# Where the second MoE splits its token operands: between the output products, or one pair ahead inside the first product

## The chip, the cores and the metric

The kernel runs on one core of one Trainium2 chip. The metric is the device time of one execution in microseconds (us), the median of several runs. Engines are named as the profile names them: PE is TensorE (PEld its weight loads), DVE is VectorE, ACT is ScalarE, POOL is GpSimd, SP is SyncE, whose queue issues most of the transfers.

## The reference

```python
x = masked_attention(q, k, v)                  # 4 x 8 heads, 576 positions, 64 wide; as 2304 tokens x 512
h = x @ w_in;  x = (h - np.tanh(h)) @ w_out    # first MoE: 512 -> 2048 -> 512
h = x @ w_in2                                  # second MoE: 512 -> 1024
e = np.exp(h - h.max(-1, keepdims=True))
solu = h * e / (e.sum(-1, keepdims=True) + 1e-09)
ln = (solu - mean(solu)) / np.sqrt(var(solu) + 1e-06) * g_ln
out = ln @ w_out2                              # 1024 -> 512, float32
```

Everything is float32. The kernel keeps that precision on TensorE by writing each operand as a high and a low part in a rounded format (`fp32r`) and adding three products: high x high, high x low, low x high.

## The kernel before, in words

The program is one stream per engine, written out in order; each engine runs its own stream in that order, and a wait of one instruction holds everything behind it on the same engine.

**First MoE.** 2304 tokens are six groups of 384; a slot `s` is one of 16 blocks of the hidden width of a group. In slot `s` TensorE does `mm1` (12 matmuls into a bank `h`, of which there are two) and `mm2` of five slots earlier (12 matmuls into the four banks `y`). ACT does the tanh (L362), VectorE the subtraction `t` (L365), which frees the bank `h`, ACT the high part `gs` (L368), VectorE the low part (L371). At the end of a group `y` goes to a DRAM buffer `y_dr`.

In the last group (slots NS-NF to NS-1, sixteen of them) the weights of the second MoE are prepared beside this, one block per slot: a load (L444), ACT's `top` (L449), VectorE's `f` (L457), ACT's high part (L473), VectorE's low part (L479). GpSimd makes four differences of weight blocks per half (L467, in two steps of two); they belong to a scheme that needs seven products of blocks in place of eight.

**The split of tokens.** A pair is 256 tokens, two tiles of 128; there are nine. `load_y(j)` fetches the pair `j` from `y_dr` into `yr` (one buffer). `split_y(j)` prepares the operands `yt` (two buffers): GpSimd makes three sums and differences `ysm` and overwrites one quarter of `yr` with a fourth (L530), VectorE casts the high parts (L535: `yr` first tile, `yr` second tile, `ysm`), GpSimd subtracts for the low parts (L536, one behind each cast). The second cast reads the quarter that the fourth addition writes. Pairs 0 and 1 are split during the last group of the first MoE, the others between the output products.

**Second MoE.** `mm3(i)` is the first product of a pair: seven blocks of 6 matmuls (`sp`, L618), in banks `b0` to `b3`. ACT copies `b0` to `c` (L650); VectorE adds `u2` (L651, from `b1` and `c`) and `u3` (L656, from `b3` and `u2`) and combines them with later banks into the negated `hn` of each tile (L634). The sixth block, `b21`, overwrites the bank `b3` that `u3` reads, so it waits for `u3`. Then, per tile, the odd one first: exponential (ACT, L678), product (VectorE, L683), mean and its subtraction (L689, L690), and `fac`: ACT's Square (L697) and six small operations on GpSimd (L699 to L704) that give the row factor `f`.

`trz` transposes a tile's `hn` on TensorE into two banks `zt` (L714, 8 matmuls); ACT copies the high part `zh` (L716), VectorE subtracts for the low part `zl` (L717), which frees the bank. `mm4` is the output product (`po`, L727, 24 matmuls), scaled by `f` in ACT's `o` (L730) and stored (L731).

The order of the main loop for pair `i` is: split of pair i+2, load of pair i+3, `mm4` odd, `trz` odd of pair i+1, `mm4` even, `trz` even of pair i+1, `mm3(i+2)`. The first two pairs differ: `mm3(0)` and `mm3(1)` follow each other, and `trz` of both tiles of pair 0 stands inside `mm3(1)` (its `mid`).

## Time and profile before

| | |
|---|---|
| median of 3 runs | 734.07 us (731.76 to 735.8) |
| the profiled execution's own time | 735.53 us |
| its span | 733.7 us |
| PE busy | 702.3 us (96%) |
| PEld | 645.5 us (88%) |
| DVE | 459.3 us (63%) |
| ACT | 367.7 us (50%) |
| POOL | 185.6 us (25%) |

The profile and the trace are of one execution, and its rows are in microseconds from the start of its span. A busy share says little by itself here: TensorE is never far from busy, so what matters is where it waits, and on whom. A matmul's shown length holds the drain of the pipeline, so lengths of neighbouring rows overlap a little; differences of starts do not have that fault. A row of the windows view gives, for each engine, the busy time in a stretch and the number of instructions, then the granted clock of TensorE (1.00 is 2.4 GHz, 0.50 is 1.2 GHz). A row of a timeline ends with the idle time ahead of it and who ended it, where there was any.

### The profile page before, as it was taken

How to read it: one execution, taken by the hardware profiler on the slowest of the kernel's cores; microseconds unless marked ns; L12 is line 12 of the kernel's file. 1: busy time of each engine (PE TensorE's matmuls, PEld its weight loads, DVE VectorE, ACT ScalarE, POOL GpSimd, SP SyncE). 2: the span in 40 equal slices, each digit the busy share in tenths (PEclk: the TensorE clock that was granted, in tenths of full speed). 3: DMA queues.
4: the chain of work that ended last, by engine and by line, in shares of the span. 5: the costliest groups of instructions: out<-in, count | busy, mean ns of one | idle time of the engine just before them, and what ended most of it. 6: DMA issues, size and time to landing. Idle time of an engine off the chain costs nothing. (4 is left out here: it accounts for less than half of the span.)

```text
span 733.7 us, 11467 instructions
## 1 busy us (share of the span) xinstructions
PE 702.3 (96%) x4106; PEld 645.5 (88%) x4106; DVE 459.3 (63%) x1157; ACT 367.7 (50%) x917; POOL 185.6 (25%) x253
## 2 busy tenths in 40 slices
PE   6888999999999999999999999899999999999997
PEld 5688899999999999999999999899778777877786
DVE  5987676476676667776666335969665545554550
ACT  5778775465556555555554334544343234323431
POOL 2212311011110101111111101743263456345620
PEclk9999999999999999999999999899999999999999
DMA  9985521132223222212130016332101110111001
GB/s 273 339 271 177 181 69 54 64 109 65 66 65 108 66 66 65 90 55 64 64 108 1 1 58 205 125 115 88 44 0 58 57 58 1 58 59 58 29 15 43
DMA packets 30312, 64.03 MB, mean 87 GB/s; under 512 B 2992, under 2 KB 16816, under 8 KB 30256
## 3 DMA queue, kind: packets, MB, share of 16 engines
q1 hardware_dynamic: 27088, 58.59, 25.3%
q10 hardware_dynamic: 3168, 4.72, 1.8%
q8 instruction: 32, 0.52, 0.3%
q14 instruction: 24, 0.20, 0.1%
HBM read 53.86 MB, written 9.44 MB: 86 GB/s over the span
## 5 line engine op out<-in xcount | busy, mean ns | idle before, releaser
L354 PE MATMUL h<-x,wi 128*128 128x384 f32 x1152 | 223.7, 343 | 4.4 <-DVE t L365 4.3
L381 PE MATMUL y<-gs,wo 128*128 128x384 f32 x1152 | 219.2, 340 | 0.0
L354 PEld LDWEIGHTS h<-x,wi 128*128 128x128 f32 x1152 | 200.7, 190 | 6.4 <-DVE t L365 5.3
L381 PEld LDWEIGHTS y<-gs,wo 128*128 128x128 f32 x1152 | 201.6, 190 | 1.8
L253 POOL TENSOR_TENSOR p<-p,rs 96x512 f32<-96x512 f32 x47 | 57.3, 1219 | 352.0 <-DVE rs L251 330.2
L371 DVE TENSOR_TENSOR gs<-t,gs 128x384 fp32r<-128x384 f32 x96 | 78.8, 821 | 42.4 <-ACT gs L368 42.3
L727 PE MATMUL po<-w2o_o,z 128*128 128x512 f32 x432 | 102.6, 394 | 0.0
L365 DVE TENSOR_TENSOR t<-h,t 128x384 f32<-128x384 f32 x96 | 53.0, 552 | 70.6 <-ACT t L362 70.6
L727 PEld LDWEIGHTS po<-w2o_o,z 128*128 128x128 f32 x432 | 80.5, 188 | 17.3
L362 ACT ACTIVATE t<-h 128x384 f32<-128x384 f32 x96 | 46.8, 488 | 82.8 <-PE h L354 79.7
L245 ACT ACTIVATE p<-p,nm 96x128 f32<-96x128 f32 x192 | 75.1, 393 | 21.3 <-DVE nm L210 21.0
L368 ACT CAST gs<-t 128x384 fp32r<-128x384 f32 x96 | 48.6, 507 | 46.7 <-DVE t L365 46.6
L678 ACT ACTIVATE e<-hn,sml 128x1024 f32<-128x1024 f32 x18 | 20.8, 1153 | 67.1 <-DVE sml L634 50.5
L618 PE MATMUL sp<-w2i_t,yt 128*128 128x512 f32 x216 | 52.4, 396 | 0.9 <-DVE u L651 0.9
L618 PEld LDWEIGHTS sp<-w2i_t,yt 128*128 128x128 f32 x216 | 40.4, 188 | 11.0 <-DVE u L651 1.4
L618 PE MATMUL sp<-w2i_b,yt 128*128 128x512 f32 x162 | 41.2, 399 | 0.0
L535 DVE CAST yt<-yr 128x512 fp32r<-128x512 f32 x18 | 15.0, 843 | 37.3 <-POOL yr L530 37.3
L205 PE MATMUL qkp<-qkr 64*96 64x128 f32 x160 | 29.4, 339 | 7.3 <-DMA qkr<-in_qk_dram 5.4
L245 ACT ACTIVATION_READ_ACCUMULATOR p<-p,nm 96x1 f32 x192 | 36.3, 189 | 0.0
L618 PEld LDWEIGHTS sp<-w2i_b,yt 128*128 128x128 f32 x162 | 29.8, 188 | 6.5
L205 PEld LDWEIGHTS qkp<-qkr 64*96 64x96 f32 x160 | 24.1, 205 | 11.9 <-DMA qkr<-in_qk_dram 5.8
L730 ACT ACTIVATE o<-po,sml 128x512 f32<-128x512 f32 x18 | 12.2, 679 | 42.8 <-POOL yt L536 25.0
(82 smaller groups left out, 845.0 us busy)
## 6 DMA issues: line engine op xcount, KB each, us to landing
qkr<-in_qk_dram SPq DMA_DIRECT2D x28, 448.0 KB, 3.3
raw_wi<-in_w_in_dram SPq DMA_DIRECT2D x16, 511.8 KB, 7.2
raw_wo<-in_w_out_dram SPq DMA_DIRECT2D x16, 511.8 KB, 7.0
v<-in_vw_dram SPq DMA_DIRECT2D x48, 128.0 KB, 3.4
y_dr<-ys ACTq DMA_DIRECT2D x6, 768.0 KB, 3.9
yr<-y_dr SPq DMA_DIRECT2D x9, 512.0 KB, 4.5
out_dram<-o SPq DMA_DIRECT2D x18, 256.0 KB, 4.5
qkr<-in_qk_dram SPq DMA_DIRECT2D x20, 224.0 KB, 4.5
```

The lines of the kernel that those rows point to most:

```text
L205: nc.tensor.matmul(ps[:, b], d["r"][:64, b * NQ:(b + 1) * NQ], d["r"][:64, QC + b * NK:QC + (b + 1) * NK], start=True, stop=True)
L245: nc.scalar.activation(out=d["p"][:, b], in_=d["p"][:, b], func=AF.Exp, scale=-1.0, bias=d["nm"][:, b:b + 1], accum_out=d["sm"][:, b:b + 1])
L253: eng.tensor_tensor(out=d["p"], in0=d["p"], in1=d["rs"].unsqueeze(2).to_broadcast([NQ, 4, NK]), op=ALU.mult)
L354: nc.tensor.matmul(ps, w[:, a, k * 128:(k + 1) * 128], xt[g, k][:, b], start=(n == 0), stop=(n == 3 * KD - 1))
L362: nc.scalar.activation(out=t, in_=ps, func=AF.Tanh)
L365: nc.vector.tensor_tensor(out=t, in0=ps, in1=t, op=ALU.subtract)
L368: nc.scalar.copy(out=gs[:, 0], in_=t)
L371: nc.vector.tensor_tensor(out=gs[:, 1], in0=t, in1=gs[:, 0].bitcast(F32), op=ALU.subtract)
L381: nc.tensor.matmul(yb[g][m], wo[c][:, a, m * 128:(m + 1) * 128], gs[:, b], start=(c == 0 and i == 0), stop=(c == NF - 1 and i == 2))
L618: nc.tensor.matmul(ps, y[:, a, blk, kk], w2i[w, kk][:, b], start=first and q == 0, stop=q == 5, skip_group_check=not first)
L678: nc.scalar.activation(out=d["e"], in_=d["hn"], func=AF.Exp, bias=d["sml"][:, 0:1], scale=-1.0, accum_out=d["sml"][:, 1:2])
L727: nc.tensor.matmul(po, z[:, a, j], w2o[j][:, b], start=(q == 0), stop=(q == 3 * NF2 - 1))
```

## The change

1. In the last group of the first MoE, the load of pair 0 moves to the group's start and its split from slot 7 to slot 3; the split of pair 1 moves from slot 14 to slot 8. Each is followed by the load of the next pair.
2. `split_y` takes parts. From pair 2 on, a pair is split inside the first product of the pair ahead of it: part 0 (three additions, cast and low part of the first tile) behind the second block, parts 1 and 2 (fourth addition, the other two casts and low parts) behind `u2`, and then the load of the next pair. The low part of the first tile now stands ahead of the fourth addition on GpSimd. In the main loop the split is gone.
3. `fac` is taken out of `softmax_z`. That of the odd tile stays where it was; that of the even tile is issued behind `trz` of the odd tile, so its Square stands on ACT behind the odd tile's `zh`.

```diff
--- before.py
+++ after.py
@@ -507,7 +507,7 @@
 
     w2_plan()
 
-    yt, y_raw = {}, {}
+    yt, y_raw, y_sm = {}, {}, {}
 
     NP = NTOK // YT
 
@@ -516,25 +516,31 @@
             y_raw[j] = p2.tile([128, KD, YT], F32, tag="yr", name=f"yr{j}", bufs=1)
             nc.sync.dma_start(out=y_raw[j], in_=y_dr[:, :, j * YT:(j + 1) * YT])
 
-    def split_y(j):
+    def split_y(j, parts=range(3)):
 
         if j >= NP:
             return
-        r = y_raw.pop(j)
-        y = p2.tile([128, 2, 7, 2, TT], F32R, tag="yt", name=f"yt{j}")
-        sm = p2.tile([128, 3, 2, TT], F32, tag="ysm", name=f"ysm{j}", bufs=1)
-        a11, a12 = r[:, 0:2, 0:TT], r[:, 2:4, 0:TT]
-        a21, a22 = r[:, 0:2, TT:YT], r[:, 2:4, TT:YT]
-        for o, a, b, op in ((sm[:, 0], a21, a22, ALU.add), (sm[:, 1], sm[:, 0], a11, ALU.subtract),
-                            (sm[:, 2], a11, a21, ALU.subtract), (a21, a12, sm[:, 1], ALU.subtract)):
-            nc.gpsimd.tensor_tensor(out=o, in0=a, in1=b, op=op)
+        r = y_raw[j]
+        if 0 in parts:
+            y = yt[j] = p2.tile([128, 2, 7, 2, TT], F32R, tag="yt", name=f"yt{j}")
+            sm = y_sm[j] = p2.tile([128, 3, 2, TT], F32, tag="ysm", name=f"ysm{j}", bufs=1)
+            a11, a21, a22 = r[:, 0:2, 0:TT], r[:, 0:2, TT:YT], r[:, 2:4, TT:YT]
+            for o, a, b, op in ((sm[:, 0], a21, a22, ALU.add), (sm[:, 1], sm[:, 0], a11, ALU.subtract),
+                                (sm[:, 2], a11, a21, ALU.subtract)):
+                nc.gpsimd.tensor_tensor(out=o, in0=a, in1=b, op=op)
+        y, sm = yt[j], y_sm[j]
+        if 1 in parts:
+            nc.gpsimd.tensor_tensor(out=r[:, 0:2, TT:YT], in0=r[:, 2:4, 0:TT], in1=sm[:, 1], op=ALU.subtract)
         yh = y[:, 0].rearrange("p s k t -> p (s k) t")
         yl = y[:, 1].rearrange("p s k t -> p (s k) t")
-        for sl, v in ((slice(0, 4), r[:, :, 0:TT]), (slice(4, 8), r[:, :, TT:YT]),
-                      (slice(8, 14), sm.rearrange("p s k t -> p (s k) t"))):
-            nc.vector.tensor_copy(out=yh[:, sl], in_=v)
-            nc.gpsimd.tensor_tensor(out=yl[:, sl], in0=v, in1=yh[:, sl].bitcast(F32), op=ALU.subtract)
-        yt[j] = y
+        for p, sl, v in ((0, slice(0, 4), r[:, :, 0:TT]), (2, slice(4, 8), r[:, :, TT:YT]),
+                         (1, slice(8, 14), sm.rearrange("p s k t -> p (s k) t"))):
+            if p in parts:
+                nc.vector.tensor_copy(out=yh[:, sl], in_=v)
+                nc.gpsimd.tensor_tensor(out=yl[:, sl], in0=v, in1=yh[:, sl].bitcast(F32), op=ALU.subtract)
+        if 2 in parts:
+            y_raw.pop(j)
+            y_sm.pop(j)
 
 
     p2 = None
@@ -555,6 +561,7 @@
             p2 = tc.alloc_tile_pool(name="p2", bufs=2, side="right", reuse_waits="tile")
             nc.gpsimd.tensor_scalar(out=gl2, in0=gl_sb, scalar1=256.0, scalar2=None, op0=ALU.mult)
             w2_load(0)
+            load_y(0)
             w2_load(1)
         for half in range(2):
             if ys_p is None and not (wq or wld or wa or wf or wh):
@@ -587,14 +594,10 @@
                 fn()
             nxt = follow
             slot += 1
-        if s == NS - NF + 4:
-            load_y(0)
-        if s == NS - NF + 7:
-            split_y(0)
-            load_y(1)
-        if s == NS - NF + 14:
-            split_y(1)
-            load_y(2)
+        for j, d in ((0, 3), (1, 8)):
+            if s == NS - NF + d:
+                split_y(j)
+                load_y(j + 1)
     for fn in nxt:
         fn()
     assert not w2s, sorted(w2s)
@@ -643,12 +646,17 @@
         b0, b1 = bank(sa, "b0", i, "p1"), bank(sa, "b1", i, "p6")
         prod(b0, y, 0, "b11")
         prod(b1, y, 5, "t2")
+        if i > 0:
+            split_y(i + 1, (0,))
         u2 = p3.tile([128, 512], F32, tag="u2", name=f"u2_{i}", bufs=1)
         u3 = p3.tile([128, 512], F32, tag="u3", name=f"u3_{i}", bufs=1)
         b2, b3 = bank(sb, "b2", i, "p5"), bank(sb, "b3", i, "p7")
         c = p3.tile([128, 512], F32, tag="c", name=f"c_{i}", bufs=1)
         nc.scalar.copy(out=c, in_=b0)
         nc.vector.tensor_tensor(out=u2, in0=b1, in1=c, op=ALU.add)
+        if i > 0:
+            split_y(i + 1, (1, 2))
+            load_y(i + 2)
         prod(b2, y, 4, "t1")
         if 0 in mid:
             mid[0]()
@@ -669,6 +677,7 @@
         neg_add(i, 0, 1, b2, u2)
         softmax_e(2 * i)
         softmax_z(2 * i + 1)
+        fac(2 * i + 1)
         softmax_u(2 * i)
         softmax_z(2 * i)
 
@@ -688,7 +697,6 @@
         usum, nmean = d["sml"][:, 2:3], d["sml"][:, 3:4]
         nc.vector.tensor_scalar(out=nmean, in0=usum, scalar1=-1.0 / FF2, scalar2=None, op0=ALU.mult)
         nc.vector.tensor_scalar(out=d["hn"], in0=d["hn"], scalar1=nmean, scalar2=None, op0=ALU.add)
-        fac(i)
 
     def fac(i):
         d = st[i]
@@ -731,13 +739,12 @@
         nc.sync.dma_start(out=out[i * TT:(i + 1) * TT, :], in_=o)
 
     mm3(0)
-    mm3(1, {0: lambda: trz(1), 1: lambda: trz(0)})
+    mm3(1, {0: lambda: (trz(1), fac(0)), 1: lambda: trz(0)})
     for i in range(NP):
-        split_y(i + 2)
-        load_y(i + 3)
         mm4(2 * i + 1)
         if i + 1 < NP:
             trz(2 * i + 3)
+            fac(2 * i + 2)
         mm4(2 * i)
         if i + 1 < NP:
             trz(2 * i + 2)
```

What stands on VectorE around the `zl` copies and the first product of pair 6, before (`zt11`, `zt10` are the transposes of the odd and even tile of pair 5, `sp6_6` and `sp7_6` banks of the product of pair 6):

```order
L690 TENSOR_SCALAR hn10_6522<-hn10_6522,sml10_6523 128x1024
L535 CAST yt6_6556<-yr6_6380 128x512 x2
L535 CAST yt6_6556<-ysm6_6557 128x768
L717 TENSOR_TENSOR z11_6598<-zt11_0_6599,z11_6598 128x512
L717 TENSOR_TENSOR z11_6598<-zt11_1_6606,z11_6598 128x512
L717 TENSOR_TENSOR z10_6641<-zt10_0_6642,z10_6641 128x512
L717 TENSOR_TENSOR z10_6641<-zt10_1_6649,z10_6641 128x512
L651 TENSOR_TENSOR u2_6_6670<-sp6_6_6657,c_6_6674 128x512
L656 TENSOR_TENSOR u3_6_6671<-sp7_6_6673,u2_6_6670 128x512
```

Here the three casts, which are for the pair whose product follows, stand ahead of all four `zl`. On VectorE at the same place, in the change:

```order
L699 TENSOR_SCALAR hn10_6536<-hn10_6536,sml10_6537 128x1024
L725 TENSOR_TENSOR z11_6590<-zt11_0_6591,z11_6590 128x512
L725 TENSOR_TENSOR z11_6590<-zt11_1_6598,z11_6590 128x512
L725 TENSOR_TENSOR z10_6641<-zt10_0_6642,z10_6641 128x512
L725 TENSOR_TENSOR z10_6641<-zt10_1_6649,z10_6641 128x512
L539 CAST yt7_6670<-yr7_6501 128x512
L656 TENSOR_TENSOR u2_6_6677<-sp6_6_6657,c_6_6681 128x512
L539 CAST yt7_6670<-yr7_6501 128x512
L539 CAST yt7_6670<-ysm7_6671 128x768
L664 TENSOR_TENSOR u3_6_6678<-sp7_6_6680,u2_6_6677 128x512
```

The four `zl` now follow the softmax directly; one cast stands ahead of `u2` and two ahead of `u3`, and they are for the pair after.

On VectorE in the second pair, where `mm3(1)` holds the transposes of pair 0 (`zt1` odd, `zt0` even), before:

```order
L690 TENSOR_SCALAR hn0_5652<-hn0_5652,sml0_5653 128x1024
L651 TENSOR_TENSOR u2_1_5700<-sp6_1_5687,c_1_5704 128x512
L717 TENSOR_TENSOR z1_5713<-zt1_0_5714,z1_5713 128x512
L717 TENSOR_TENSOR z1_5713<-zt1_1_5721,z1_5713 128x512
L656 TENSOR_TENSOR u3_1_5701<-sp7_1_5703,u2_1_5700 128x512
L634 ISA hn3_5735,sml3_5736<-sp5_1_5702,u3_1_5701 128x512
L634 ISA sml3_5736 128x1
L634 ISA hn3_5735,sml3_5736<-sp4_1_5738,u3_1_5701,sml3_5736 128x512
L634 ISA sml3_5736 128x1
L717 TENSOR_TENSOR z0_5746<-zt0_0_5747,z0_5746 128x512
L717 TENSOR_TENSOR z0_5746<-zt0_1_5754,z0_5746 128x512
```

No cast stands here; those of pair 2 come behind this pair's softmax. On VectorE at the same place, in the change:

```order
L699 TENSOR_SCALAR hn0_5652<-hn0_5652,sml0_5653 128x1024
L539 CAST yt2_5692<-yr2_5208 128x512
L656 TENSOR_TENSOR u2_1_5699<-sp6_1_5679,c_1_5703 128x512
L539 CAST yt2_5692<-yr2_5208 128x512
L539 CAST yt2_5692<-ysm2_5693 128x768
L725 TENSOR_TENSOR z1_5719<-zt1_0_5720,z1_5719 128x512
L725 TENSOR_TENSOR z1_5719<-zt1_1_5727,z1_5719 128x512
L664 TENSOR_TENSOR u3_1_5700<-sp7_1_5702,u2_1_5699 128x512
L637 ISA hn3_5749,sml3_5750<-sp5_1_5701,u3_1_5700 128x512
L637 ISA sml3_5750 128x1
L637 ISA hn3_5749,sml3_5750<-sp4_1_5752,u3_1_5700,sml3_5750 128x512
L637 ISA sml3_5750 128x1
```

The casts of pair 2 now stand here, one ahead of `u2` and two ahead of the `zl` of tile 1 and of `u3`.

On GpSimd in the last group of the first MoE, before (L467 are the differences of weight blocks, `yr0` and `yr1` the tokens of pairs 0 and 1):

```order
L467 TENSOR_TENSOR t3_0_5069<-f3_5029,f1_4946 128x512
L467 TENSOR_TENSOR f1_4946<-f1_4946,f0_4908 128x512
L530 TENSOR_TENSOR ysm0_5140<-yr0_5010 128x256
L530 TENSOR_TENSOR ysm0_5140<-ysm0_5140,yr0_5010 128x256
L530 TENSOR_TENSOR ysm0_5140<-yr0_5010 128x256
L530 TENSOR_TENSOR yr0_5010<-yr0_5010,ysm0_5140 128x2x128
L536 TENSOR_TENSOR yt0_5139<-yr0_5010,yt0_5139 128x512 x2
L536 TENSOR_TENSOR yt0_5139<-ysm0_5140,yt0_5139 128x768
L467 TENSOR_TENSOR f3_5029<-f3_5029,f1_4946 128x512
L467 TENSOR_TENSOR f2_4983<-f2_4983,f3_5029 128x512
L467 TENSOR_TENSOR t3_1_5331<-f9_5295,f7_5218 128x512
```

The first split stands between the two steps of the first half's differences. On GpSimd at the same place, in the change:

```order
L530 TENSOR_TENSOR ysm0_4970<-yr0_4826 128x256
L530 TENSOR_TENSOR ysm0_4970<-ysm0_4970,yr0_4826 128x256
L530 TENSOR_TENSOR ysm0_4970<-yr0_4826 128x256
L533 TENSOR_TENSOR yr0_4826<-yr0_4826,ysm0_4970 128x2x128
L540 TENSOR_TENSOR yt0_4969<-yr0_4826,yt0_4969 128x512 x2
L540 TENSOR_TENSOR yt0_4969<-ysm0_4970,yt0_4969 128x768
L467 TENSOR_TENSOR t3_0_5083<-f3_5043,f1_4948 128x512
L467 TENSOR_TENSOR f1_4948<-f1_4948,f0_4910 128x512
L467 TENSOR_TENSOR f3_5043<-f3_5043,f1_4948 128x512
L467 TENSOR_TENSOR f2_4999<-f2_4999,f3_5043 128x512
L530 TENSOR_TENSOR ysm1_5197<-yr1_4981 128x256
L530 TENSOR_TENSOR ysm1_5197<-ysm1_5197,yr1_4981 128x256
```

The first split now stands ahead of both steps, and the second split, which stood behind all eight differences, follows the first four.

## Rows read from the trace of the kernel before

**Rows 1.** Windows view, four stretches: width, busy us (count) of PE, PEld, DVE, ACT, POOL, clock, DMA.

```profile
598.57:622.92 24.35, 22.94 (x109) 18.46 (x108) 13.20 (x25) 8.65 (x16) 12.22 (x22) 1.00 0.14 44
696.02:718.58 22.56, 22.56 (x109) 18.57 (x108) 11.00 (x22) 8.21 (x15) 6.04 (x15) 1.00 0.03 12
535.16:549.85 14.69, 13.06 (x65) 10.49 (x64) 8.29 (x17) 5.98 (x11) 10.66 (x19) 1.00 0.00 0
705.90:718.58 12.68, 12.68 (x65) 10.59 (x64) 5.86 (x12) 5.51 (x10) 4.50 (x13) 1.00 0.05 21
```

**Rows 2.** Chain of waits in one middle pair: start us, us, what.

```profile
618.52 0.75 POOL yr L530
...
619.29 1.97 DVE yt L535 x2
```

**Rows 3.** Timeline, PE, the same pair: start us, us, instruction, count, [idle before <-releaser].

```profile
598.57 1.64 PE L618 MATMUL sp<-w2i_b,yt 128*128 128x512 f32 x6
...
605.64 2.96 PE L618 MATMUL sp<-w2i_b,yt 128*128 128x512 f32 x12
...
621.91 1.25 PE L714 MATMUL zt<-cst_sb,hn 128*128 128x128 f32 x8 [1.41 <-DVE z L717]
```

**Rows 4.** Timeline, DVE, the same pair, and one row of the last pair.

```profile
604.44 0.69 DVE L656 TENSOR_TENSOR u<-sp,u 128x512 f32<-128x512 f32 x1 [2.04 <-PE sp L618]
...
613.54 0.42 DVE L535 CAST yt<-yr 128x512 fp32r<-128x512 f32 x1
619.29 1.50 DVE L535 CAST yt<-yr 128x512 fp32r<-128x512 f32 x1 [5.33 <-POOL yr L530]
620.71 0.55 DVE L535 CAST yt<-ysm 128x768 fp32r<-128x768 f32 x1
...
719.23 1.29 DVE L717 TENSOR_TENSOR z<-zt,z 128x512 fp32r<-128x512 f32 x2 [4.52 <-ACT z L716]
```

**Rows 5.** Timeline, POOL, the same middle pair.

```profile
619.22 1.29 POOL L536 TENSOR_TENSOR yt<-yr,yt 128x512 fp32r<-128x512 f32 x1
620.87 1.52 POOL L536 TENSOR_TENSOR yt<-yr,yt 128x512 fp32r<-128x512 f32 x1 [0.36 <-DVE yt L535]
```

**Rows 6.** Timeline, ACT, the last pair.

```profile
718.04 0.69 ACT L730 ACTIVATE o<-po,sml 128x512 f32<-128x512 f32 x1 [4.16 <-issue]
...
718.62 1.06 ACT L716 CAST z<-zt 128x512 fp32r<-128x512 f32 x2
```

**Rows 7.** Timeline, PE, end of the first stage.

```profile
473.88 4.21 PE L354 MATMUL h<-x,wi 128*128 128x384 f32 x12 [2.96 <-DVE t L365]
...
480.84 2.28 PE L354 MATMUL h<-x,wi 128*128 128x384 f32 x12
...
485.08 2.28 PE L354 MATMUL h<-x,wi 128*128 128x384 f32 x12
...
497.80 2.28 PE L354 MATMUL h<-x,wi 128*128 128x384 f32 x12
```

**Rows 8.** Windows view, one stretch behind the stall of the first stage.

```profile
474.00:478.00 4.00, 4.00 (x13) 4.00 (x14) 3.90 (x8) 2.73 (x6) 0.00 (x0) 0.50 0.00 0
```

**Rows 9.** Timeline, DVE, beside the first split and beside the second.

```profile
467.80 2.33 DVE L479 SCALAR_TENSOR_TENSOR w2o_o<-f,gl,w2o_o 128x512 fp32r<-128x512 f32 x1
...
504.82 0.54 DVE L365 TENSOR_TENSOR t<-h,t 128x384 f32<-128x384 f32 x1
```

**Rows 10.** Timeline, POOL, behind the first split.

```profile
469.55 3.39 POOL L467 TENSOR_TENSOR f<-f,f 128x512 f32<-128x512 f32 x2
```

**Rows 11.** Timeline, PE, the second pair.

```profile
529.99 1.66 PE L618 MATMUL sp<-w2i_t,yt 128*128 128x512 f32 x6 [0.94 <-DVE u L651]
...
535.16 5.66 PE L727 MATMUL po<-w2o_o,z 128*128 128x512 f32 x24
```

**Rows 12.** Timeline, POOL, last operation on the odd tile's factor before the second pair.

```profile
526.94 1.00 POOL L704 TENSOR_TENSOR sml<-sml 128x1 f32<-128x1 f32 x1
```

**Rows 13.** The page's DMA issues: KB each, median us from issue to landing.

```profile
yr<-y_dr SPq DMA_DIRECT2D x9, 512.0 KB, 4.5
```

## The prediction

> **What bounds the kernel now.** I read the page first, then the second MoE stage by windows, by the chain of waits and by the timelines of its engines, and last the end of the first MoE stage by timeline and windows.
>
> TensorE is busy nearly everywhere, so what can be won is the little time in which it waits. The second stage repeats one period per pair of tiles: the first product (`sp`, 42 matmuls), an output product (`po`, 24), the odd tile's transposes (`zt`), `po` again, the even tile's `zt`. In a middle period TensorE is busy 22.94 of 24.35 us; in the last one, which splits no tokens, the same 109 instructions take 22.56 without a gap, and GpSimd is busy 6.04 in place of 12.22 [rows 1]. So a period has 1.79 us of wait. The chain says which: the last of GpSimd's four additions of the split, then VectorE's casts [rows 2], then the subtraction `zl` of the odd tile (L717), then the even tile's `zt`, which needs the `zt` bank that `zl` reads. The timelines show the rest: `zt` starts after 1.41 us of idle on `z` L717 [rows 3]; VectorE did its first cast at once (0.42), sat 5.33 us in front of the second until GpSimd's fourth addition, took 1.50 for it and 0.55 for the third, and only then reached `zl` [rows 4].
>
> The stall at the end of the first stage is the other loss. TensorE idles 2.96 us at 473.88, and its next 24 matmuls take 6.96 us (473.88 to 480.84) where the 24 behind them take 4.24 (to 485.08) [rows 7]: the granted clock was 0.50 there, which is 1.2 GHz [rows 8]. VectorE was the cause: beside GpSimd's subtractions one of its operations took 2.33 us [rows 9], and GpSimd's two differences for the weights, queued behind the whole first split, ran only from 469.55 [rows 10]. Wait and slow clock: 2.96 + 2.72 = 5.7 us.
>
> **The change part by part.** It adds and removes no instruction; it moves them. I call M the start of a pair's first `sp` matmul.
>
> *Seven waits removed.* The split of the next pair now stands inside the first product, so `zl` of the odd tile follows the softmax directly. Six full periods (third pair to ninth) lose 24.35 - 22.56 = 1.79 each: 10.7. The period before them loses 14.69 - 12.68 = 2.0, its stretch from the first `po` on against the same stretch of the last pair [rows 1]. Together 12.7. The Square that moves behind the odd tile's copies costs nothing: its result is used one period later.
>
> *What is late next, in a full period.* VectorE must now do a cast, the sum `u2`, two casts, and then `u3` on time: `u3` starts at M+5.87 (604.44 - 598.57) [rows 3, 4], and TensorE's `b21` product, which overwrites the bank that `u3` reads, starts at M+7.07 (605.64) [rows 3]. With 0.69 for `u3`, 0.5 us are free. The gap-free last pair shows where VectorE stands at the start: counted from 718.58, where a next first product would begin, `o` runs from -0.54, the copies `zh` from 0.04 [rows 6], `zl` from 0.65 to 1.94 [rows 4]. First cast to M+2.4; GpSimd, whose three additions are done long before, subtracts (1.29 [rows 5]) to 3.7 and does the fourth addition (0.75 [rows 2]) to 4.5; second cast to 5.0, third (0.55) to 5.5. That is 0.4 before `u3` can start, so 0.9 before TensorE would wait. I take 0. The cover is TensorE's 18 matmuls between `u2`'s banks and `u3`'s; without it, each microsecond that the casts end late beyond M+6.4 is lost once per pair.
>
> Here a rule of the Trainium skill speaks against the change. The rows first: a cast takes 0.42 alone and 1.50 beside GpSimd's 1.29 us subtraction [rows 4, 5], a surcharge of 1.08; `zl`, which reads PSUM, takes 1.29 for two whether GpSimd works or not. I take no surcharge, since GpSimd waits for the first two casts while they run, and in the old order the third cast won against the next subtraction (0.55 [rows 4], GpSimd starting at 620.87 [rows 5]). GPSIMD Engine Reference, 8. Key points, says that GpSimd shares its SBUF interfaces with VectorE and contends with its instructions in a two-port mode or with two SBUF inputs; the trace agrees, by the 1.08. Taken for every cast it would make the sum the last rival's, below.
>
> *The second pair (head).* Here the new place is bad. The odd tile's `zl` and the transposes of the even tile lie in the middle of this pair's first product, behind the casts. GpSimd comes free at 526.94 + 1.00 = 527.94 [rows 12]; three additions (2.3) to 530.2, subtraction 531.5, fourth addition 532.25, two casts 533.2, two `zl` 533.85 and 534.5, `u3` 535.2. TensorE could start `t4` 0.94 us earlier than its 529.99 (the old wait, `u2` behind a Square, is gone) [rows 11] and so stands idle from 530.4 to 533.85, 3.5 us, in front of the even tile's transposes; `b21` waits for `u3`, 12 matmuls (2.8) follow, and `po` starts at 538.0 in place of 535.16 [rows 11]: +2.85. A pause of 2.96 was followed by the half clock [rows 7, 8], one of 1.41 was not, so I add the 2.7 that it cost there. Head: +5.6, with 2.9 (no half clock) and 0 (GpSimd earlier) as lower ends.
>
> *First stage.* The first split moves four slots earlier, where GpSimd was idle, in front of the first two weight differences; the second split moves six slots earlier, behind the other two. Its old place had the same neighbours on VectorE one round of weights later, so the old rows price it: the last subtraction of the activation ends at 504.82 + 0.54 [rows 9], 7.6 after its slot's first matmul at 497.80 [rows 7]. A bank is needed two slots later, 8.4 by the same pitch, so 0.8 are free. I take a gain of 5.2 of the 5.7 and leave 0.5 for either split using up its margin; bounds 0 and 5.7.
>
> *Loads.* They move with the splits. The first token load now goes out between the first two weight loads, so that the second waits behind it; the weights of that step are converted one slot later, and I cost it at nothing. In the pairs a load goes out when GpSimd has read the old tokens for the last time, about M+8.4, lands 4.5 us later [rows 13], and is read near M+19; the output stores stand behind it on the queue as before. Without that cover the load's 4.5 would be lost per pair.
>
> *Sum.* -12.7 - 5.2 + 5.6 = -12.3 on the profiled execution's 735.5 gives 723.2. That execution lies 1.5 above the median 734.07, so 721.7; I say 722.
>
> **The rivals.**
> 1. *The third cast loses to GpSimd's next subtraction.* It then starts 1.3 later and ends at M+6.8, `u3` at 7.5, and TensorE waits 0.4 in six pairs (2.4); the head gets 1.3 longer. 723.2 + 3.7 = 726.9, median 725.4. For it: the cast that took 1.50 did wait; against: the third did not.
> 2. *The first-stage stall only changes its place.* VectorE is already dense there and the second split meets slots with as many weight operations. 723.2 + 5.2 = 728.4, median 726.9. For it: the 2.33 us operation; against: the 0.8 us margin of the old second split.
> 3. *The wait moves whole.* If `u3` held TensorE 1.8 us per pair, the six periods stay: 723.2 + 10.7 = 733.9, median 732.4: no change. It needs the casts to end at M+8.2.
> 4. *Slower: every cast collides.* Three times 1.08 per pair puts the casts' end at M+8.7 and `u3` at 9.4; TensorE waits 2.35 in six pairs (14.1) and 3.2 more in the head: 723.2 + 17.3 = 740.5, median 739.0. It decides from about 2.1 us of wait per pair. Against it: GpSimd has nothing else to do while the first two casts run.
>
> **How the numbers follow.** Chances: forecast 0.64 (its own range 717 to 724: without the half clock 719, without the 0.5 and with a shorter pause 717, with small waits in the pairs 724), rival 1 0.14, rival 2 0.12, rival 3 0.05, rival 4 0.05. The range 716 to 728 holds the first three. Half a per cent (3.7 us) is about what a measurement of this kernel tells from no change: faster 0.90, same 0.05, slower 0.05.
>
> **What would show it.** Right: periods of about 22.6 us; `zt` of both tiles without idle time; the third cast ended before the `b3` product; one pause of 3 us or more in the second pair, before `zt`, with the granted clock at 1.2 GHz behind it; no pause near 470. Wrong: idle time on TensorE before `b21` in every pair, released by `u3`; a cast of 1.3 us or more in the new place; a wait of `h` on `t` in the first stage. The forecast fails most likely by a collision of GpSimd with VectorE that the old order does not show.

## The result, and the profile after

| | before | after |
|---|---|---|
| median (range) | 733.49 us (731.76 to 735.8, 4 runs) | 722.38 us (721.08 to 723.21, 4 runs) |
| ratio, 95% interval | | 0.9845 (0.9812 to 0.9878) |
| profiled execution, its span | 735.53 us, 733.7 us | 723.21 us, 721.4 us |

The change makes the kernel faster by 11 us (1.5%), 0.4 us from the forecast. The busy shares and the chain that ended last, by engine, from the page after:

```profile
PE 699.2 (97%) x4106; PEld 644.9 (89%) x4106; DVE 452.7 (63%) x1157; ACT 366.2 (51%) x917; POOL 184.9 (26%) x253
...
PE 85%; DVE 8%; issue 2%; DMA 2%; ACT 2%; POOL 1%; SPq 0%; POOLq 0%; ACTq 0%; DVEq 0%
```

No engine does much less than before; what changed is the chain. In the page of before PE held 17% of it, now 85%: the end follows TensorE nearly everywhere. The windows view after, on stretches that answer to [rows 1]: a middle period, a last one, the stretch from the first `po` to the third pair, and the head (start of the first pair's product to the first `po`):

```profile
548.46:571.00 22.54, 22.54 (x109) 18.55 (x108) 12.21 (x25) 8.47 (x16) 12.22 (x21) 1.00 0.14 47
683.74:706.29 22.55, 22.55 (x110) 18.57 (x108) 10.98 (x22) 8.47 (x16) 4.71 (x13) 1.00 0.06 24
535.78:548.46 12.68, 12.68 (x66) 10.59 (x64) 5.35 (x12) 5.52 (x10) 5.89 (x15) 1.00 0.05 21
509.20:535.78 26.58, 23.39 (x101) 18.49 (x101) 16.33 (x35) 9.60 (x17) 13.08 (x23) 0.94 0.15 50
```

In the first three PE is busy for the whole width, although GpSimd works 12.22 us in a middle period, as long as before. In the head PE is not. A middle pair in PE's timeline, with no idle time at either `zt` (against [rows 3]):

```profile
548.46 1.64 PE L621 MATMUL sp<-w2i_b,yt 128*128 128x512 f32 x6
...
555.53 2.96 PE L621 MATMUL sp<-w2i_b,yt 128*128 128x512 f32 x12
...
563.83 1.03 PE L722 MATMUL zt<-cst_sb,hn 128*128 128x128 f32 x8
...
570.21 1.03 PE L722 MATMUL zt<-cst_sb,hn 128*128 128x128 f32 x8
```

The same pair on VectorE, and then on GpSimd (against [rows 4, 5]):

```profile
550.33 0.42 DVE L539 CAST yt<-yr 128x512 fp32r<-128x512 f32 x1
551.60 0.69 DVE L656 TENSOR_TENSOR u<-sp,c 128x512 f32<-128x512 f32 x1 [0.86 <-PE sp L621]
552.91 0.43 DVE L539 CAST yt<-yr 128x512 fp32r<-128x512 f32 x1 [0.62 <-POOL yr L533]
553.25 0.55 DVE L539 CAST yt<-ysm 128x768 fp32r<-128x768 f32 x1
554.33 0.69 DVE L664 TENSOR_TENSOR u<-sp,u 128x512 f32<-128x512 f32 x1 [0.53 <-PE sp L621]
```

```profile
550.89 1.29 POOL L540 TENSOR_TENSOR yt<-yr,yt 128x512 fp32r<-128x512 f32 x1 [3.21 <-DVE yt L539]
552.14 0.74 POOL L533 TENSOR_TENSOR yr<-yr,ysm 128x256 f32<-128x256 f32 x1
553.42 1.54 POOL L540 TENSOR_TENSOR yt<-yr,yt 128x512 fp32r<-128x512 f32 x1 [0.54 <-DVE yt L539]
```

The third cast, begun 0.17 us ahead of GpSimd's subtraction, keeps its 0.55; the casts end at 553.80, which is M+5.34 (M = 548.46, the start of the pair's first `sp` matmul); `u3` waits only for PE and starts at M+5.87, as before.

The head on PE, then on VectorE, then the window behind the pause:

```profile
530.21 1.31 PE L722 MATMUL zt<-cst_sb,hn 128*128 128x128 f32 x8 [3.19 <-DVE z L725]
531.40 4.54 PE L621 MATMUL sp<-w2i_b,yt 128*128 128x512 f32 x12
535.78 5.67 PE L735 MATMUL po<-w2o_o,z 128*128 128x512 f32 x24
```

```profile
528.66 0.43 DVE L539 CAST yt<-yr 128x512 fp32r<-128x512 f32 x1 [3.67 <-POOL yr L533]
529.00 0.55 DVE L539 CAST yt<-ysm 128x768 fp32r<-128x768 f32 x1
529.47 1.28 DVE L725 TENSOR_TENSOR z<-zt,z 128x512 fp32r<-128x512 f32 x2
```

```profile
530.30:535.60 5.30, 5.30 (x20) 4.09 (x21) 4.94 (x11) 2.41 (x4) 4.65 (x12) 0.68 0.36 104
```

TensorE waits 3.19 us for `zl`, which stands behind casts that wait for GpSimd, and the granted clock behind the wait is 0.68 (a part of it at 1.2 GHz): the 12 matmuls of the sixth and seventh block (`b21` and `b22`) take 4.38 us from start to start. `b21` starts when `u3` ends (530.67 + 0.68 on VectorE), 1.19 us behind the start of `zt`.

The first stage on PE: the stall of [rows 7] is gone, and two smaller waits are there, the first for VectorE's copies `ys` of the banks `y` at the end of a group, the second for the subtraction `t`.

```profile
452.75 2.36 PE L381 MATMUL y<-gs,wo 128*128 128x384 f32 x12 [0.46 <-DVE ys L387]
...
477.30 2.38 PE L354 MATMUL h<-x,wi 128*128 128x384 f32 x12 [1.37 <-DVE t L365]
```

Where the 12.3 us between the spans went, by starts of PE's rows. Slot 80 is the first slot of the last group of the first MoE; it starts at 429.16 before and 429.25 after.

| stretch | before | after | difference |
|---|---|---|---|
| slot 80 to the first pair's product | 83.48 | 79.95 | -3.5 |
| head: first pair's product to first `po` | 22.52 | 26.58 | +4.1 |
| first `po` to the third pair's product | 14.69 | 12.68 | -2.0 |
| six periods | 146.2 | 135.3 | -10.9 |

### The profile page after: what moved, and what is told of

It is laid out like the page before. It is cut to its first block, busy times and chain, and to the rows that moved or that the text cites. A ratio compares the mean times of both kernels' runs of the same rounds, so it can differ in the third digit from the quotient of the medians.

```text
span 721.4 us, 11466 instructions
## 1 busy us (share of the span) xinstructions
PE 699.2 (97%) x4106; PEld 644.9 (89%) x4106; DVE 452.7 (63%) x1157; ACT 366.2 (51%) x917; POOL 184.9 (26%) x253
## 4 chain that ended last, share of the span: by engine, by line
PE 85%; DVE 8%; issue 2%; DMA 2%; ACT 2%; POOL 1%; SPq 0%; POOLq 0%; ACTq 0%; DVEq 0%
PE y L381 26%; PE h L354 24%; PE po L735 14%; PE sp L621 11%; PE zt L722 2%; PE pv L281 2%; PE qkp L225 2%; PE tp L260 2%; PE qkp L205 2%; DMA raw_w<-in_w_in_dram 1%; DVE p L210 1%; DVE wy_wi L129 1%; DVE gs L371 1%; DVE wi L104 1%; DMA qkr<-in_qk_dram 1%
## 5 line engine op out<-in xcount | busy, mean ns | idle before, releaser
L371 DVE TENSOR_TENSOR gs<-t,gs 128x384 fp32r<-128x384 f32 x96 | 81.1, 845 | 35.7 <-ACT gs L368 35.7
L245 ACT ACTIVATE p<-p,nm 96x128 f32<-96x128 f32 x192 | 75.1, 393 | 21.2 <-DVE nm L210 20.9
L725 DVE TENSOR_TENSOR z<-zt,z 128x512 fp32r<-128x512 f32 x36 | 23.2, 685 | 55.3 <-ACT z L724 55.3
L205 PEld LDWEIGHTS qkp<-qkr 64*96 64x96 f32 x160 | 24.1, 205 | 11.7 <-DMA qkr<-in_qk_dram 5.7
```

What stands on the lines that cost most here:

```text
L205: nc.tensor.matmul(ps[:, b], d["r"][:64, b * NQ:(b + 1) * NQ], d["r"][:64, QC + b * NK:QC + (b + 1) * NK], start=True, stop=True)
L245: nc.scalar.activation(out=d["p"][:, b], in_=d["p"][:, b], func=AF.Exp, scale=-1.0, bias=d["nm"][:, b:b + 1], accum_out=d["sm"][:, b:b + 1])
L371: nc.vector.tensor_tensor(out=gs[:, 1], in0=t, in1=gs[:, 0].bitcast(F32), op=ALU.subtract)
L725: nc.vector.tensor_tensor(out=zl, in0=ps, in1=zh.bitcast(F32), op=ALU.subtract)
```

## The experiments

All are timed in the same way, each against runs of the kernel before on the same chip (medians 732.8, 732.3 and 734.0 us in the three series). The last three columns come from PE's rows: slot 80 to the first pair's product, the head, and a middle period. A kernel's early part alone differs by up to 2.1 us between profiled executions (slot 80 starts at 427.7 to 429.8 us), so medians less than 2 us apart are read by these columns. The first stage's column differs too where its code is the same: 79.1 to 79.95 in the six traces with its splits at slots 3 and 8 (the change, 2, 3, 5, 6, 7), and 83.5 and 81.0 in the two with the old places (before, 1).

After the two traces my theory (A) was that the period of before hung on GpSimd's queue: the split's additions stood behind the even tile's factor, which waits for its Square, so that either move of the change would take the wait away. The rivals (B, C) hold that only one of the two moves does it. Later expectations carry their theories with them; "group 3" in them is slot 3 of the last group of the first MoE.

| kernel | us (range) | ratio to before | first stage | head | period |
|---|---|---|---|---|---|
| before | 733.49 (731.76 to 735.8) | | 83.5 | 22.5 | 24.35 |
| the change | 722.38 (721.08 to 723.21) | 0.9845 (0.9812 to 0.9878) | 79.95 | 26.6 | 22.55 |
| 1 Square alone | 719.78 (718.01 to 721.4) | 0.982 (0.9798 to 0.9842) | 81.0 | 21.3 | 22.55 |
| 2 splits alone | 724.88 (722.0 to 725.07) | 0.9875 (0.9854 to 0.9897) | 79.6 | 28.5 | 22.55 |
| 3 no split in the head | 720.45 (720.22 to 721.05) | 0.9831 (0.9815 to 0.9847) | 79.7 | 21.3 | 22.55 |
| 4 second split late | 720.68 (718.7 to 722.01) | 0.9822 (0.9802 to 0.9841) | 78.7 | 26.0 | 22.55 |
| 5 one more subtraction | 725.09 (724.7 to 725.94) | 0.9896 (0.988 to 0.9913) | 79.1 | 27.8 | 22.95 |
| 6 two more | 735.63 (735.1 to 737.18) | 1.0038 (1.0023 to 1.0052) | 79.6 | 28.9 | 24.33 |
| 7 Square and first stage | 717.92 (717.48 to 719.24) | 0.9797 (0.9779 to 0.9814) | 79.65 | 21.3 | 22.55 |
| 8 as 7, second split late | 715.37 (714.37 to 717.02) | 0.9761 (0.9742 to 0.978) | 77.6 | 21.3 | 22.55 |
| 9 first split early | 721.39 (719.75 to 723.32) | 0.9836 (0.9809 to 0.9863) | 78.8 | 25.1 | 22.55 |
| 10 as 8, first split early | 714.33 (713.33 to 718.39) | 0.9751 (0.9723 to 0.9779) | 77.0 | 21.3 | 22.55 |

**1. The Square alone.** The kernel before with the third part of the change only; every split stays in its old place.

```diff
+        fac(2 * i + 1)               # in mm3; out of softmax_z
...
-    mm3(1, {0: lambda: trz(1), 1: lambda: trz(0)})
+    mm3(1, {0: lambda: (trz(1), fac(0)), 1: lambda: trz(0)})
...
             trz(2 * i + 3)
+            fac(2 * i + 2)
```

> The kernel before with the third part of the change alone: the Square and the factor of the even tile are issued behind the odd tile's z copies, every split stays where it was. Theory A (the pair's wait is the tail of GpSimd's queue: the split stands behind the even tile's six factor operations, and the casts hold zl): the split starts about 2.0 us earlier, right behind the odd tile's factor, which is more than the 1.79 us of wait, so the periods fall to about 22.6 us, the old 0.94 us wait of the second pair goes too, the stall of the first stage stays: about 720 us. Theory B (the split has to leave the place between the output products, as the change's first part says): periods stay at 24.35 us, about 733 us.

The whole gain per pair is there without moving a split. GpSimd's timeline says why; first before, then in this kernel, the last operation on the odd tile's factor and the split's first addition of one pair:

```profile
613.07 0.99 POOL L704 TENSOR_TENSOR sml<-sml 128x1 f32<-128x1 f32 x1
...
616.17 0.74 POOL L530 TENSOR_TENSOR ysm<-yr 128x256 f32<-128x256 f32 x1
```

```profile
602.85 1.00 POOL L704 TENSOR_TENSOR sml<-sml 128x1 f32<-128x1 f32 x1
603.82 0.72 POOL L530 TENSOR_TENSOR ysm<-yr 128x256 f32<-128x256 f32 x1
```

Before, the seven small operations on the even tile's factor (the six of L699 to L704 and a memset) stood between the two, and the additions began 616.17 - 598.57 = 17.6 us after the pair's first matmul; here they begin at once, at 603.82 - 588.34 = 15.5. Those 2.1 us are more than the 1.79 that the period lost. The second cast still takes 1.50 beside GpSimd's subtraction (606.91 in this trace), but `zl` now comes in time.

**2. The splits alone.** The change with `fac` back in its old place, at the end of `softmax_z`.

```diff
-        fac(2 * i + 1)
...
+        fac(i)                       # in softmax_z
...
-    mm3(1, {0: lambda: (trz(1), fac(0)), 1: lambda: trz(0)})
+    mm3(1, {0: lambda: trz(1), 1: lambda: trz(0)})
...
-            fac(2 * i + 2)
```

> The changed kernel without its third part: Square and factor of the even tile directly behind its mean, splits one pair ahead as in the change. Theory A: the periods stay at 22.55 us, since nothing of the pair waits for the split any more; in the second pair the split starts behind the even tile's factor too, 2 us later, so the pause there grows from 3.2 to about 5.3 us: about 724.5 us. Theory C (the Square's place is a part of the gain in every pair, by ACT reaching the z copies sooner): periods of more than 22.6 us, 728 us or more.

The periods are 22.55 us here too, so either move alone takes the wait away. The head is the worst but one of all. Two rows of PE's timeline:

```profile
526.34 1.67 PE L621 MATMUL sp<-w2i_t,yt 128*128 128x512 f32 x6 [0.94 <-DVE u L656]
532.13 1.96 PE L722 MATMUL zt<-cst_sb,hn 128*128 128x128 f32 x8 [4.12 <-DVE z L725]
```

The Square ahead of `c` brings back the old wait for `u2` (0.94, [rows 11]). The split's additions stand behind the even tile's factor and begin 17.4 us after the pair's first matmul (526.40 - 508.99), where they began after 15.25 with the change; the pause is 4.12 us. I had expected one pause of 5.3; the two waits add up to 5.06.

**3. No split in the head.** The change, with pair 2 split in the old place (between the output products, and pair 3 loaded behind it).

```diff
-        if i > 0:
+        if i > 1:                    # both places in mm3
...
+        if i == 0:
+            split_y(2)
+            load_y(3)
```

> The changed kernel, but pair 2 is split where it was before (behind the second product, between the output products); pairs 3 to 8 as in the change. Theory A (the casts of pair 2 ahead of tile 1's zl cause the pause of the second pair and the half clock behind it): no pause, the granted clock stays at 1.00, the stretch from the first product to the first output product falls from 26.6 to about 21.5 us, the next stretch stays at 12.7: about 717.5 us. Rival (the pause comes from the softmax of the first pair, which is late anyway): a pause of 2 us or more stays, 720 us or more.

The pause in the head is gone (21.3 us), but only 2 us come back: a new wait is in the third pair. SyncE's queue, VectorE and PE there, and the window behind the wait:

```profile
540.63 0.53 SPq L517 DMA_DIRECT2D yr<-y_dr  x1
```

```profile
545.20 0.43 DVE L539 CAST yt<-yr 128x512 fp32r<-128x512 f32 x1 [1.49 <-DMA yr<-y_dr]
...
549.70 0.43 DVE L539 CAST yt<-yr 128x512 fp32r<-128x512 f32 x1 [3.47 <-POOL yr L533]
550.05 0.55 DVE L539 CAST yt<-ysm 128x768 fp32r<-128x768 f32 x1
550.51 0.68 DVE L664 TENSOR_TENSOR u<-sp,u 128x512 f32<-128x512 f32 x1
```

```profile
551.25 4.50 PE L621 MATMUL sp<-w2i_b,yt 128*128 128x512 f32 x12 [2.26 <-DVE u L664]
```

```profile
551.30:555.50 4.20, 4.20 (x12) 3.34 (x13) 2.67 (x7) 1.24 (x2) 3.33 (x6) 0.63 0.44 126
```

There is one `yr` buffer, so the load of pair 3 goes out only when pair 2 is split, at 540.63; the tokens are there only at 545.2, so GpSimd's additions come late too; the casts end at 550.60, M+8.9 (M = 541.75), and TensorE waits 2.26 us for `u3`. With the lower clock behind it the pair loses 4.0. My 717.5 had left the load out.

**4. The second split late.** The change with the second split at slot 14 of the last group, its old place.

```diff
-        for j, d in ((0, 3), (1, 8)):
+        for j, d in ((0, 3), (1, 14)):
```

> The changed kernel, but pair 1 is split after slot 14 as before, not after slot 8. Theory A (each split costs where VectorE is dense; the 1.4 us wait of the first stage belongs to the second split, the 0.5 us wait to the first): the wait at the sixth bank before the end goes, the one on the y copies stays: 1.5 us less than the change, about 721 us. Rival (the wait belongs to the first split, which delays everything behind it): the wait stays, 722.4 us.

The wait of 1.37 us at 477 is gone, the one for the copies of `y` (0.48) stays, and the first stage is 1.2 us shorter than in the change's trace (0.3 to 1.0 shorter than in the other five with that split). So the wait at 477 belongs to the second split at slot 8.

**5 and 6. How much room the casts have.** The change with GpSimd's first subtraction of the split issued once or twice more from pair 2 on; it writes the same values again.

```diff
-                nc.gpsimd.tensor_tensor(out=yl[:, sl], in0=v, in1=yh[:, sl].bitcast(F32), op=ALU.subtract)
+                for _ in range(2 if p == 0 and len(parts) == 1 else 1):
+                    nc.gpsimd.tensor_tensor(out=yl[:, sl], in0=v, in1=yh[:, sl].bitcast(F32), op=ALU.subtract)
```

> This is the changed kernel with GpSimd's first subtraction of tokens (yl of part 0) issued twice inside the first product, from the second pair on; the second one writes the same values again. It lengthens GpSimd's queue ahead of the fourth addition by one subtraction, 1.29 us in the changed kernel's trace. Theory A (there is slack: the last cast ends 5.34 us after the start of the pair's first product, and TensorE would wait only from 6.4 on): the casts end at 6.6, so each of the six pairs loses about 0.25 us (1.5 in all) and the pause at the second pair grows from 3.2 to 4.5 us (+1.3): about 725.2 us, periods of 22.8 us. Rival S (no slack at all, whatever delays GpSimd here delays the pair): 7 times 1.29, 731.4 us, periods of 23.85. Rival N (GpSimd is not on this path): only the pause at the second pair grows, 723.7 us, periods of 22.55.

> As the kernel with one repeated subtraction, with two (2.58 us more on GpSimd ahead of the fourth addition). Theory A (1.06 us of slack): the casts end 7.9 us after the start of the pair's first product, each pair loses about 1.5 us, with a wait of TensorE on VectorE's u3 ahead of the b21 product, and the pause at the second pair grows to 5.8 us: 722.4 + 6 x 1.5 + 2.6, about 734 us, periods of about 24.1 us, slower if the clock also falls behind the new waits. Rival S (no slack): 722.4 + 7 x 2.58, 740.5 us. Rival N: only the second pair, 725.0 us, periods of 22.55.

With two more, GpSimd and PE in a middle pair, and the window behind the wait:

```profile
577.09 4.06 POOL L541 TENSOR_TENSOR yt<-yr,yt 128x512 fp32r<-128x512 f32 x3 [3.20 <-DVE yt L539]
```

```profile
583.42 3.06 PE L622 MATMUL sp<-w2i_b,yt 128*128 128x512 f32 x12 [1.52 <-DVE u L665]
```

```profile
559.10:562.00 2.90, 2.90 (x13) 2.36 (x14) 2.13 (x6) 1.23 (x2) 2.32 (x3) 1.00 0.33 87
```

GpSimd's queue is 4.06 - 1.29 = 2.77 us longer and the period 1.78, so 0.99 were free. With one more (2.66 for two, 1.37 longer) the period grows by 0.40, so 0.97 were free. One microsecond is the whole margin of the new order; beyond it each of the six pairs pays in full, and 2.8 us more on GpSimd make the kernel slower than before. The first time came out as theory A has it (725.1 us, 725.2 expected), the second 1.6 above it (735.6, about 734 expected; the period is 24.33, not 24.1). Both are far from no slack at all (731.4 and 740.5) and from no path at all (723.7 and 725.0 us). The wait is at `b21` for `u3`, as expected, and this wait of 1.5 us leaves the clock at 1.00.

**7. The Square and the first stage.** Experiment 1 with the first load and the first two splits where the change puts them.

```diff
             w2_load(0)
+            load_y(0)
             w2_load(1)
...
+        for j, d in ((0, 3), (1, 8)):
+            if s == NS - NF + d:
+                split_y(j)
+                load_y(j + 1)
```

> The kernel before with the Square of the even tile moved as in the change, and the first two splits and the first load put where the change puts them (end of groups 3 and 8, load at the start); the splits of the later pairs stay between the output products. Against the kernel with the Square alone (719.8 us) it shows what the first stage's part of the change is worth. My prediction's term of 5.2 us would give 714.6. Theory A (term mis-sized: two waits of 0.5 and 1.4 us stay, so the stage gains about 3.5 against the profile of before, and 1 to 3.5 against the kernel with the Square alone, whose own wait there was 2.3 us): 716.3 to 718.8. Rival (the wait only moves, nothing gained): 719.8. The periods stay at 22.55 us and the second pair at 21.3.

It differs from the change only in where, and in which order, pairs 2 to 8 are split and loaded, and is 4.5 us faster in the medians (3.5 by the ratios to before). The head is the place; the window on it, without a gap (against 26.58 us after the change):

```profile
508.71:530.04 21.33, 21.33 (x102) 17.44 (x101) 14.90 (x32) 9.41 (x17) 5.44 (x16) 1.00 0.11 38
```

Against experiment 1 the first stage gives 1.9 us (medians; 1.4 by the column), within what theory A has.

**8. The second split late as well.** As 7, with the second split at slot 14.

```diff
-        for j, d in ((0, 3), (1, 8)):
+        for j, d in ((0, 3), (1, 14)):
```

> As the kernel with the Square and the first stage's splits, but with the second split at the end of group 14 instead of 8. In the changed kernel this move took the wait of 1.4 us at the second split away (79.95 to 78.7 us from slot 80 to the first product, 1.2 to 1.7 us of the time). Theory A: 1.2 to 1.7 us less than the kernel with the second split at group 8, 714.8 to 717.3 us, with no wait of TensorE in the first stage but 0.5 us on the copies of y, and the fastest of all kernels run. Rival: the split and the weight arithmetic near group 14 collide as in the kernel before, and the wait of 2 to 3 us with half the clock behind it comes back, 719.8 us.

715.37 us, 7.0 less than the change (6.2 by the ratios); one wait of TensorE is left between slot 80 and the last pair, 0.36 us for the copies of `y`.

**9. The first split early.** The change with the first split at slot 2.

```diff
-        for j, d in ((0, 3), (1, 8)):
+        for j, d in ((0, 2), (1, 8)):
```

> The changed kernel with the first split one group of weights earlier (end of group 2 in place of 3); the second split stays at group 8. It asks why VectorE reaches the second split 2.2 us later in its slot than I took from the old place. Theory C (the first split's subtractions on GpSimd slow VectorE's weight arithmetic in front of the copies of y at 452, ScalarE waits for those copies 3 us, and all its later work of the stage is late): the wait of 0.46 us in front of the y product goes, and the wait of 1.4 us at the second split shrinks below 0.5: 1.5 to 2 us less than the change, about 720.6 us. Rival L (the lateness comes from the weight loads alone): the wait of 1.4 us stays, 0.5 us less at most, about 722.0 us.

Of theory C only the copies' part holds: the wait for them is gone. The wait at the second split is 1.01, not under 0.5. In the other traces with the second split at slot 8 and the first at slot 3 it is 0.74 to 1.13 (experiments 2, 3, 5, 6 and 7) and 1.37 (the change), so 1.01 is what it is without any move of the first split. VectorE's timeline says the same. Two subtractions `t` and the five operations between them, in front of the second split, in this kernel:

```profile
462.84 0.54 DVE L365 TENSOR_TENSOR t<-h,t 128x384 f32<-128x384 f32 x1
463.31 1.31 DVE L479 SCALAR_TENSOR_TENSOR w2i_t<-t,w2i_t 128x512 fp32r<-128x512 f32 x1
464.55 1.22 DVE L479 SCALAR_TENSOR_TENSOR w2i_t<-f,w2i_t 128x512 fp32r<-128x512 f32 x1
465.69 1.23 DVE L479 SCALAR_TENSOR_TENSOR w2o_o<-f,gl,w2o_o 128x512 fp32r<-128x512 f32 x1
466.85 1.22 DVE L457 SCALAR_TENSOR_TENSOR f<-raw_w,top 128x512 int32<-128x512 int32 x1
467.99 1.10 DVE L371 TENSOR_TENSOR gs<-t,gs 128x384 fp32r<-128x384 f32 x1
469.01 0.55 DVE L365 TENSOR_TENSOR t<-h,t 128x384 f32<-128x384 f32 x1
```

The same two subtractions in experiment 7, with the first split at slot 3:

```profile
462.91 0.54 DVE L365 TENSOR_TENSOR t<-h,t 128x384 f32<-128x384 f32 x1
469.08 0.54 DVE L365 TENSOR_TENSOR t<-h,t 128x384 f32<-128x384 f32 x1
```

The first of them starts 0.24 us ahead of the next slot's first matmul here (463.08), 0.14 ahead in experiment 7 (463.05), and 0.14 to 0.29 ahead in experiments 2, 3, 5 and 6. The five operations last 6.08 us, beside GpSimd's weight differences and additions (460.91 to 468.67); in experiment 10, which has no split there, 3.95 (the three in the middle 0.68, 0.74 and 0.68).

The change's own trace is the odd one. There ScalarE's `top` waits 1.10 us for a weight load, which it does in none of the five others:

```profile
462.25 0.80 ACT L449 ACTIVATE top<-raw_w 128x512 f16<-128x512 bf16 x1 [1.10 <-DMA raw_w<-in_w_in_dram]
```

Behind it the first subtraction starts 1.23 us after the next slot's first matmul (464.51 and 463.28), and the five operations last 4.98. So moving the first split takes away the wait for the copies and no more. The wait at the second split stays, as rival L has it; that the weight loads alone make VectorE late is not shown, since the five other traces have the wait of TensorE without this one of `top`.

**10. The best order, first split early.** As 8, with the first split at slot 2.

```diff
-        for j, d in ((0, 3), (1, 14)):
+        for j, d in ((0, 2), (1, 14)):
```

> The fastest kernel so far (715.4 us: Square moved, first two splits at the ends of groups 3 and 14, later splits in the old place) with the first split at the end of group 2. Theory C: the wait of TensorE for the copies of y (0.36 us) goes, so 715.0 us, with no wait of TensorE left between slot 80 and the last pair; from slot 80 to the first product of the second stage 77.3 us. Rival L: the same, since only the small wait differs; if the tokens are not there yet at group 2, GpSimd and VectorE wait for the load and the stage loses 1 us or more, 716.5 us.

No wait is left on TensorE from slot 80 to the first pair's product; the window on all of it:

```profile
427.71:504.67 76.96, 76.96 (x446) 76.96 (x445) 56.05 (x82) 39.41 (x74) 29.45 (x23) 1.00 0.42 141
```

714.33 us has the lowest median of all. Its range (713.33 to 718.39) holds that of experiment 8, so the times don't tell these two apart. The column is 0.6 us shorter, of which 0.36 is the wait that is gone; the rest is within what traces of the same code differ by.

## Why the prediction was right, and where by luck

The time was right because two of the three terms were off by nearly the same amount in opposite directions. By the traces the sum is -12.9 - 3.5 + 4.1 = -12.3, against -12.7 - 5.2 + 5.6 = -12.3. The medians lie 11.1 apart, since the profiled execution of before was 2.0 above its median and that of after 0.8; I had taken off 1.5 for this.

*Seven waits removed (-12.7).* Measured: -10.9 in six periods and -2.0 in the stretch ahead of them. The size was right. The cause was read too narrowly. I followed the chain of waits back to the fourth addition [rows 2] and put its lateness down to the split's place; one step further back stood the even tile's factor in GpSimd's queue. "The Square that moves behind the odd tile's copies costs nothing" was true, and missed that this small move wins the whole term by itself (experiment 1), as does the move of the split (experiment 2).

*What is late next (0).* Right, within 0.2 us. I had the casts ending at M+5.5 and 0.9 us free; they end at M+5.34, and experiments 5 and 6 measure 0.97 and 0.99 free. The loads were rightly costed at nothing, and experiment 3 shows the price without their cover: 4.0 us in the one pair whose load came late.

*The head (+5.6, measured +4.1).* The mechanism was right in each step: `zt` was released 21.0 us after the first pair's start (I had 21.2), the pause is 3.19 (3.5), and it ends with `zl`. The half clock was mis-sized: I took 2.7 from the stall of the first stage; here the 12 matmuls behind `u3` take 4.38 us, where experiment 7 has 2.88, so 1.5. That is most of what was off; the rest is 0.4 in GpSimd's and VectorE's chain, where I had `u3` end at 535.2, 22.6 after the first pair's start, against 22.15. Measured against an order without this split (experiment 7), it costs 26.58 - 21.33 = 5.25 us.

*The first stage (-5.2, measured -3.5).* This is the step that failed: "its old place had the same neighbours on VectorE one round of weights later, so the old rows price it". They did price the work: from one subtraction `t` to the next, with the casts between, VectorE takes 7.13 us after the change (469.57 to 476.70) and took 7.15 at the old place (497.67 to 504.82). But it began the stretch 2.13 us behind the next slot's first matmul (467.44), where at the old place it began 0.13 ahead of it (497.80). So the last subtraction ended 9.8 us after that matmul, not 7.6, and TensorE waited 1.37. I carried the duration over and not the phase. The weight load that `top` waited for in this trace (experiment 9) is not the reason: in the five other traces with these two splits VectorE began 1.65 to 1.88 behind, and TensorE waited 0.74 to 1.13. The phase is lost ahead of the casts. The five weight operations there took 4.89 us at the old place (493.07 to 497.67) and take 6.1 at the new one in those traces, and VectorE begins them later in its slot: the subtraction in front of them starts 0.14 to 0.29 ahead of the next slot's first matmul, at the old place 0.95 ahead (492.61 and 493.56). The other 0.46 us of wait is for the copies of `y`: I had looked for a split's price on the bank `h` alone.

And the 5.7 was one execution's loss. In experiment 1, whose first stage is that of before, the wait was 2.33 us, the 24 matmuls behind it took 5.74, and the stretch was 81.0 us, not 83.5; so the first stage's gain is 3.5 in the pair of traces that I forecast from, and 1.9 by the medians of experiments 1 and 7.

*The rivals.* Rivals 1, 3 and 4 did not come: the third cast took 0.55, and no `b21` waited. Experiment 6 brings rival 3's wait about: 1.78 us per pair, all gain gone. Rival 2 came in part; 1.8 us of waits remain of the first stage's.

*What stays open.* Why the clock fell behind the pause after the change and not behind the same pause in experiment 9 (below); and why VectorE comes to the second split's new place later in its slot than to the old one.

## What to carry to other kernels

When a chain of waits ends at an operation of an in-order engine, read what stands ahead of it in that engine's queue before moving the operation: here seven small operations on another tile's factor were the delay, and moving them alone won as much as the whole change or more (719.8 us against 722.4, ratios to before 0.982 and 0.9845, whose intervals overlap; the head 5.3 us shorter, without the new pause). When an old place is used to price a new one, carry the phase as well as the duration: how far behind its slot the engine is when the work begins. And one order for all pairs is not the best order for the first: the place that is free in the steady state cost 5.25 us in the head, where the work around it is another.

## What the runs showed of the hardware

The length of a pause alone did not decide the clock behind it. The same 12 matmuls behind a pause of 3.18 us in experiment 9, in PE's timeline and the windows view:

```profile
529.65 1.25 PE L722 MATMUL zt<-cst_sb,hn 128*128 128x128 f32 x8 [3.18 <-DVE z L725]
```

```profile
529.70:535.00 5.30, 5.30 (x26) 4.19 (x27) 5.12 (x11) 2.42 (x4) 4.73 (x11) 1.00 0.35 104
```

The granted clock stayed at 1.00 there and fell to 0.68 after the change behind 3.19 us, with the same instructions on both sides. Behind 2.26 us in experiment 3 it was 0.63, behind 1.5 us in experiment 6 it stayed at 1.00. From the start of `zt` to the first `po` is 5.57 us after the change and 4.09 in experiment 9. So behind the same pause the clock cost 1.5 us in the one and nothing in the other, and that alone is not far below the whole range of the change's runs (2.1 us).

GpSimd's cost to VectorE depends on what GpSimd does. Two weight operations on VectorE, `w2o_o` (L479) and `f` (L457), take 0.74 and 0.68 us alone (experiment 10), 1.23 and 1.22 beside the split's additions (experiment 9), and 1.78 and 2.34 beside its subtractions, after the change:

```profile
472.27 1.78 DVE L479 SCALAR_TENSOR_TENSOR w2o_o<-f,gl,w2o_o 128x512 fp32r<-128x512 f32 x1
473.97 2.34 DVE L457 SCALAR_TENSOR_TENSOR f<-raw_w,top 128x512 int32<-128x512 int32 x1
```

In the second MoE the same subtractions cost VectorE nothing in the new order, where the casts begin first and the next instructions, `u3` (0.69) among them, took no longer than before.
